# An adaptive-layer-norm transformer block on one core: attention in units of sixteen heads by 128 queries, feed-forward in sixteen blocks of 128 rows

## The chip, the cores and the metric

The kernel runs on one core of a Trainium2 chip. TensorE (PE in the profile) multiplies matrices, VectorE (DVE), ScalarE (ACT) and GpSimd (POOL) work on tiles, SyncE (SP) issues the transfers. The metric is the device time in microseconds (us); the median of three runs of the kernel before is 1634.18 us (1631.97 to 1639.09).

## The reference

One block with 2048 rows x 512 columns, 32 heads of 16 that share one K and one V, and a gated feed-forward of width 1792:

```python
mod = (_silu(c) @ w_mod).reshape(c.shape[0], 6, 1, -1)
sa, ca, ga, sb, cb, gb = (mod[:, 0], mod[:, 1], mod[:, 2], mod[:, 3], mod[:, 4], mod[:, 5])
h = _layernorm(x) * (1 + ca) + sa
q, k, v = h @ wq, h @ wk, h @ wv                # 32 heads of 16 in q; one head in k and v
p = _softmax(q_head @ k.T * 16 ** -0.5)
x = x + ga * (concat(p @ v) @ wo)
h = _layernorm(x) * (1 + cb) + sb
x = x + gb * ((_sigmoid(h @ w_gate) * (h @ w_up)) @ w_down)
```

## The kernel before

**Precision.** Operands of most products are split into a high and a low fp16 part; a product is three terms (high by high, high by low, low by high). The exponentials P and V are f32.

**Attention.** The loop runs over 32 *units*. A unit is eight heads by 256 queries (`QU` = 256, `NU` = 4 units for each of `NQ` = 8 blocks of queries), and has 16 *steps*, one for each 128 keys: 512 steps in all. In a step TensorE makes four `sa` tiles (queries by 512 keys, for the maxima of the next unit, which VectorE takes: `a_tile`), four `st` tiles (keys by queries, of which ScalarE makes P: `st_tile`), and the sums of P by V into the bank `craw` (`pv`). ScalarE copies that bank into `cs` at a unit's end (`unit_end`); `place`, `recip` and `finish` bring it through DRAM into the layout of wo's operand, divided by the softmax's sum.

**Row halves.** TensorE works with 64 rows at a time in column tiles of 32 (`columns`, L152 to L154): while P by V uses one half of the rows, the other products use the other half, and the halves swap. At a swap `hand_over` (L166) sends a tiny matmul (`craw<-nought`) through, whose semaphore `turn` the other half waits for.

**Feed-forward.** Beside the attention each half step takes a *piece* (L1186) of the feed-forward of an earlier block of 256 rows: wo, gate and up, and down. One *term* is eight matmuls, 64 rows by 32 columns by 512, four on each row half. A `Couple` (L198) is two groups with a bank each, either two row tiles of 128 or gate and up of one tile; each sums one half of the rows into its own bank in the first leg, and changes sides in the second. `ffn_block` makes the groups of a block, `pick` and `pace` choose which comes next and how many terms a half step gets, and `defer(n, f)` sets a follow-up n steps later. wo becomes urgent 9 steps into the next block's units (`SKIP`). Its sum is evicted by VectorE (first tile) or ScalarE (second), then POOL adds x and normalises (`norm`, `norm2`), and SP transposes the fp16 rows (`h2r` into `h`); gate and up follow at least three steps (`HGAP`) after the last transpose. `g` is the gated product, transposed likewise, and down follows.

**Weights.** Gate and up are split on the chip once and written to DRAM (`wD`); `ask` and `drip` load them again from there for each block, 14 tiles of two transfers (`gw<-wD`), with seven buffers.

**Order.** On TensorE, VectorE, ScalarE and SP the program's order is kept (class `Ordered`, L143: all such instructions carry this line in the profile). Before the loop stands a hand-written list, `PLAN`: the normalisation of x, K, V, the first groups of q (`q`, `QA`, `QL`, stored to `qD` and loaded again as `qp` by `lq`), and the maxima of the first unit (`a` a product, `x` its maximum). Behind the loop the last block's wo, gate, up and down run as full 128-row matmuls (`alone`, L194), with gate and up in the transposed form `gu_cols`, and one down of the block before.

Of the kernel before, what the change touches and what calls it, by code (L numbers as in the profile page):

```python
# [24 lines left out]
QU = 256  # L25
# [4 lines left out]
NU = 4  # L30
# [34 lines left out]
EGAP = 6  # L65
HGAP = 3
CHAIN = 26
QRATE = 1.1
MOST = 3
LEAST = 2.0  # L70
HELD = 60
SWAP = 5
FRESH = 0.9
WSTEPS = 66
WLAST = 100
# [4 lines left out]
FIRST = 70  # L80
# [16 lines left out]
def adaln_mqa_glu_kernel(  # L97
# [100 lines left out]
    class Couple:  # L198
# [27 lines left out]
        def alone(self):  # L226
            for g in self.gs:
                g.alone()

# [336 lines left out]
    def blank(eng):  # L566
        qp = wp.tile([P, 4, QU], F16, tag="qp", name="qp", bufs=4)
        for j in (32, 96):
            eng.memset(qp[j:j + 32], 0.0)  # L569
        return qp  # L570

    def load_q(i):
        b, o = units[i]
        qp = blanks.pop(0) if blanks else blank(pool)
        for j in range(2):
            src = qD[:, o * P:(o + 1) * P, b * QU:(b + 1) * QU].rearrange("h (r j d) q -> j h d r q", j=2, d=DH)[j]
            for g, hl in ((0, 0), (1, 1), (2, 0)):
                spq().dma_start(qp[64 * j + 16 * g:64 * j + 16 * (g + 1)], src[hl])
# [3 lines left out]
    def get_q(i):  # L582
        if i not in qps:
            b, o = units[i]
            assert (b * QU // QB, o) in qdone
            load_q(i)
# [6 lines left out]
    def spot(n):  # L593
        return n // 16, n // 8 % 2, n % 2, n // 2 % 4

    def a_product(i, n):
        qp = get_q(i)
        if i not in mxs:
            mxs[i] = wp.tile([P, 8, 2, 4], F32, tag="mx", name="mx", bufs=2)
        kc, qt, j, r = spot(n)  # L600
        sa = sbank("sa")
        l_, r_ = qp[64 * j:64 * j + 64, r, qt * P:(qt + 1) * P], kp[64 * j:64 * j + 64, kc * 512:(kc + 1) * 512]
# [6 lines left out]
    def a_max(i, n, sa):  # L609
        kc, qt, j, r = spot(n)  # L610
        dve.tensor_reduce(mxs[i][:, 4 * j + r, qt, kc:kc + 1], sa, axis=AX.X, op=ALU.max)
# [9 lines left out]
    def max_end(i):  # L621
        m16 = wp.tile([64, 32], F32, tag="m16", name="m16", bufs=4)
        for u in range(2):
            dve.tensor_reduce(m16.rearrange("p (h t u) -> p h t u", t=2, u=2)[:, :, :, u], mxs[i][64 * u:64 * u + 64],
# [22 lines left out]
    def st_tile(i, t, pr, j, second):  # L647
# [5 lines left out]
        columns(s_, kp[64 * j:64 * j + 64, t * P:(t + 1) * P], qp[64 * j:64 * j + 64, 2 * pr:2 * pr + 2].rearrange("p r q -> p (r q)"),  # L653
# [27 lines left out]
    def unit_end(i):  # L681
# [8 lines left out]
        lD = dr.tile([2, 8, QU], F32, tag="lD", name="lD", bufs=3)  # L690
        raw = t32("raw")
        defer(1, lambda: place(b, o, cs, lD, raw))
# [3 lines left out]
    def place(b, o, cs, lD, raw):  # L696
        for j in range(2):
            sp1.dma_start(lD[0].rearrange("(p r j) q -> j p r q", j=2, r=2)[j],
                          cs[DH + 64 * j:64 + 64 * j:32].rearrange("p (r q) -> p r q", r=2))
        for g in range(8):  # L700
            p_, r_, j = g // 4, g // 2 % 2, g % 2
            hh = 2 * j + p_
            sp1.dma_start(raw[DH * g:DH * (g + 1), :QU], cs[32 * hh:32 * hh + DH, r_ * QU:(r_ + 1) * QU])
        defer(W1, lambda: recip(b, o, lD, raw))

    def recip(b, o, lD, raw):
        lc = wp.tile([P, DH], F32, tag="lc", name="lc", bufs=2)
        rc = wp.tile([P, DH], F32, tag="rc", name="rc", bufs=2)
        sp1.dma_start(lc, lD[0].rearrange("h (s e) -> (h s) e", e=DH))

        def recip2():
            dve.reciprocal(rc, lc)
            sp1.dma_start(lD[1].rearrange("h (s e) -> (h s) e", e=DH), rc)
            defer(1, recip3)

        def recip3():
            sp1.dma_start(raw[:, QU:], lD[1].unsqueeze(1).to_broadcast([8, DH, QU]))
# [4 lines left out]
    def finish(b, o, raw):  # L722
        a_ = a_tile_of()
        ah, al = a_[:, :QU], a_[:, QU:]
        keep(pool.tensor_tensor(raw[:, :QU], raw[:, :QU], raw[:, QU:], op=ALU.mult))  # L725
        pool.tensor_scalar(ah, raw[:, :QU], 1.0, 0.0, op0=ALU.mult, op1=ALU.add)
        pool.tensor_tensor(al, raw[:, :QU], ah, op=ALU.subtract)
# [577 lines left out]
```

## Time and profile before

| | |
|---|---|
| three runs | 1631.97, 1634.18, 1639.09 us |
| the profiled execution | 1629.06 us |
| its span in the trace | 1627.3 us |
| mean granted clock of TensorE | 0.993 |
| bytes moved by transfers | 140.22 MB, 86 GB/s over the span |
| start of the steps (first exponential of the long row of steps) | 105.8 us |
| end of the loop (first wo row behind it) | 1537.72 us |

The time of an execution is a little longer than the span, which goes from the first to the last instruction that the trace has. A row of the timeline gives a start, a duration, the engine, the line, the operation with out<-in and the shapes, and a count; TensorE's rows overlap, since matmuls are pipelined, so the price of a matmul is the distance of two starts. A row of a table of windows gives the window, its length, for each engine named in its head the busy time and the number of instructions, then the granted clock, the share of time that the transfer engines were busy, and GB/s.

### The profile page before, as it was taken

Reading aid. Unit: us, or ns where it says so; the run is one execution under the profiler, and the core shown is the slowest. Engines: PE = TensorE matmul, PEld = TensorE weight load, DVE = VectorE, ACT = ScalarE, POOL = GpSimd, SP = SyncE. Lnnn points to the kernel's source line nnn. Section 1 sums busy time; section 2 is a strip of 40 time slices with the busy share of each in tenths; the row PEclk is TensorE's granted clock in tenths of the full one; section 3 lists DMA queues with packets and bytes.
Section 4 is the critical chain, followed back from the end, with each engine's and each line's share of the span. In section 5 each row is a group of like instructions: output and inputs, shape, how many; then the busy total and the mean of one; then the engine's idle time right before and its main releaser. Section 6 shows DMA issues by size and latency. Waiting matters only on the chain.

```text
span 1627.3 us, 91846 instructions
## 1 busy us (share of the span) xinstructions
PE 1585.3 (97%) x41481; PEld 987.3 (61%) x41481; DVE 1417.1 (87%) x2400; ACT 1288.7 (79%) x2325; POOL 666.2 (41%) x827
## 2 busy tenths in 40 slices
PE   6899999999999999999999999999999999999998
PEld 3335554546666666666666666666666666665465
DVE  7789999999999999999999999999999999993041
ACT  4539998888888888888888888888888888888600
POOL 5453877244425332443226232543226322533223
PEclk9979999999999999999999999999999999999999
DMA  7122554044521233114321433115411343124411
GB/s 238 71 84 65 164 156 131 28 118 106 139 68 29 75 97 108 31 39 130 92 63 33 89 85 106 30 38 128 112 42 42 81 121 85 23 60 107 116 65 52
DMA packets 185076, 140.22 MB, mean 86 GB/s; under 512 B 96372, under 2 KB 144492, under 8 KB 184684
## 3 DMA queue, kind: packets, MB, share of 16 engines
q1 hardware_dynamic: 184684, 134.34, 30.4%
q8 instruction: 325, 5.32, 1.3%
q14 instruction: 67, 0.55, 0.1%
HBM read 97.18 MB, written 16.24 MB: 70 GB/s over the span
## 4 chain that ended last, share of the span: by engine, by line
PE 88%; DVE 4%; ACT 2%; DMA 2%; POOL 1%; issue 1%; SPq 1%; POOLq 0%; ACTq 0%; DVEq 0%
PE craw L143 24%; PE sa L143 18%; PE pgu L143 17%; PE st L143 11%; PE pd L143 8%; PE po L143 2%; PE pgu L194 2%; PE pq L143 2%; PE pd L194 2%; DVE mx L143 2%; ACT th L143 1%; DMA lc<-lD 1%; SPq L143 1%; DMA xall<-in_A_x_dram 1%; ACT P L143 1%
## 5 line engine op out<-in xcount | busy, mean ns | idle before, releaser
L143 DVE TENSOR_REDUCE mx<-sa 128x1 f32<-128x512 f32 x2048 | 1299.8, 683 | 69.6 <-PE sa L143 33.2
L143 ACT ACTIVATE P<-st 128x512 f32<-128x512 f32 x2048 | 1179.3, 598 | 204.7 <-PE st L143 143.7
L143 PE MATMUL craw<-P,V 64*32 64x512 f32 x8192 | 1086.0, 597 | 1.0 <-ACT cs L143 1.0
L143 PE MATMUL st<-qp,kp 64*32 64x512 f16 x8192 | 832.7, 379 | 7.3 <-ACT P L143 6.1
L143 PE MATMUL sa<-kp,qp 64*32 64x512 f16 (+1 forms) x7940 | 827.9, 378 | 8.2 <-DVE mx L143 6.2
L143 PEld LDWEIGHTS <-kp 64*32 64x32 f16 x8192 | 323.1, 91 | 249.2 <-issue 79.1
L143 PE MATMUL pgu<-gw,h 64*32 64x512 f16 x9408 | 407.4, 376 | 3.2 <-DMA gw<-wD 1.2
L143 PEld LDWEIGHTS <-qp 64*32 64x32 f16 (+1 forms) x7940 | 270.2, 92 | 149.1 <-issue 58.7
L143 PEld LDWEIGHTS <-h 64*32 64x32 f16 (+1 forms) x9600 | 212.7, 92 | 77.8 <-issue 22.6
L143 PEld LDWEIGHTS craw<-P,V 64*32 64x32 f32 x8192 | 184.4, 105 | 21.7 <-issue 2.6
L143 PE MATMUL pd<-wdh,g 64*32 64x512 f16 x2688 | 136.1, 376 | 0.7
L952 POOL TENSOR_SCALAR th<-th 128x512 f32<-128x512 f32 x49 | 30.2, 617 | 246.4 <-ACT th L143 223.2
L569 POOL MEMSET qp<- 32x1024 f16 x60 | 56.7, 944 | 118.6 <-PE st L143 100.5
L143 PEld LDWEIGHTS <-g 64*32 64x32 f16 x4032 | 82.0, 92 | 31.0 <-issue 6.5
L725 POOL TENSOR_TENSOR raw<-raw 128x256 f32<-128x256 f32 x31 | 22.7, 733 | 160.6 <-DMA raw<-lD 151.7
L143 PE MATMUL pd<-wdl,g 64*32 64x512 f16 x1344 | 80.5, 376 | 0.0
L953 POOL TENSOR_TENSOR th<-th,u 128x512 f32<-128x512 f32 x49 | 62.8, 1282 | 4.1
L1009 POOL TENSOR_TENSOR ot<-ot,gb 128x512 f32<-128x512 f32 x12 | 15.4, 1281 | 114.3 <-ACT ot L143 114.3
L143 DVE COPY u<-pgu 128x512 f32<-128x512 f32 (+1 forms) x49 | 31.6, 644 | 34.9 <-PE pgu L143 34.8
L143 PE MATMUL craw<-nought 64*32 64x1 f16 x357 | 58.2, 163 | 1.1 <-issue 1.1
L956 POOL TENSOR_TENSOR gr<-th,gr 128x512 f16<-128x512 f32 x49 | 57.1, 1165 | 4.1
L143 PE MATMUL pq<-h,wdh 64*32 64x512 f16 (+1 forms) x688 | 54.4, 390 | 0.1
(156 smaller groups left out, 1112.5 us busy)
## 6 DMA issues: line engine op xcount, KB each, us to landing
gw<-wD SPq DMA_DIRECT2D x224, 256.0 KB
wD<-gw SPq DMA_DIRECT2D x28, 256.0 KB
wm<-in_w_mod_dram SPq DMA_DIRECT2D x6, 1024.0 KB
qp<-qD SPq DMA_DIRECT2D x192, 32.0 KB
qD<-q SPq DMA_DIRECT2D x16, 256.0 KB
xr<-in_A_x_dram SPq DMA_DIRECT2D x16, 256.0 KB
out_dram<-ot SPq DMA_DIRECT2D x16, 256.0 KB
raw<-cs SPq DMA_DIRECT2D x248, 16.0 KB
```

Of the source, the lines that this page charges most:

```text
L143: return (lambda *a, **k: keep(f_(*a, **k))) if pinned else f_
L194: pe.matmul(cut[0](self.bank) if cut else self.bank, l_, r_, start=(n == 0), stop=(n == self.n - 1))
L569: eng.memset(qp[j:j + 32], 0.0)
L725: keep(pool.tensor_tensor(raw[:, :QU], raw[:, :QU], raw[:, QU:], op=ALU.mult))
L952: pool.tensor_scalar(th, th, 1.0, 1.0, op0=ALU.add, op1=ALU.mult)
L953: pool.tensor_tensor(th, th, u_, op=ALU.mult)
L956: pool.tensor_tensor(rows[:, 1], th, rows[:, 0], op=ALU.subtract)
L1009: pool.tensor_tensor(ot, ot, mods[5], op=ALU.mult)
```

## The change

The units become sixteen heads by 128 queries: still 32 units of 16 steps with the same matmuls for the attention, but two units, not four, make up a block, and the blocks have 128 rows, sixteen in all. So the feed-forward of a block starts after 32 steps, not 64, and the weights are loaded sixteen times instead of eight. wo, the last quarter of gate and up (`rest`) and down have a single row tile; a new class, `Halves`, gives each half of the rows its own bank for that tile, without a swap, and the two banks are evicted by VectorE and ScalarE and added on POOL. The other gates and ups stay Couples, gate and up of one tile. Down of a block runs after the next block's first gate and up (`block`). `place` goes through a DRAM tile `rD` with four transfers and a load, where it was eight. Behind the loop the transposes are TensorE's (`turn_alone`). Several constants and `PLAN` differ.

```diff
-QU = 256
+QU = 128
-NU = 4
+NU = 2
-    'T00 m0 S12 T01 H00 S13 E00 T02 E01 H01 L00 T03 ra1 S20 H02 E02 L01 rb1 q000 H03 E03 pk00 L02 rc1 q001 L03 pk01 '
-    'N10 q002 N11 N12 q003 N13 pk02 QA00 S21 pk03 S22 T10 QL00 KB0 S23 T11 wh1 KL0 ra2 T12 S30 H10 rb2 T13 S31 E10 '
+    'T00 m0 S12 T01 H00 S13 E00 T02 E01 wh1 H01 L00 T03 ra1 S20 H02 E02 L01 wl1 rb1 q000 H03 E03 pk00 L02 rc1 q001 '
+    'L03 pk01 N10 q002 N11 N12 q003 N13 pk02 QA00 S21 pk03 q010 q011 q012 q013 S22 T10 QL00 KB0 QA01 QL01 S23 T11 '
...
-EGAP = 6
+EGAP = 4
-CHAIN = 26
-QRATE = 1.1
+CHAIN = 24
+QRATE = 1.5
-WSTEPS = 66
-WLAST = 100
+WSTEPS = 60
+WLAST = 66
+LLATE = 2
-FIRST = 70
+FIRST = 60
...
+    class Halves:
...
+            for n in range(n0, n1):
+                for j in (1 - side[0], side[0]):
+                    columns(self.banks[j], *self.term(n, slice(64 * j, 64 * j + 64)), n == 0, n == self.n - 1)
...
+            if n1 == self.n:
+                self.end(*self.banks)
...
-        qp = wp.tile([P, 4, QU], F16, tag="qp", name="qp", bufs=4)
+        qp = wp.tile([P, 8, QU], F16, tag="qp", name="qp", bufs=4)
...
+        for hh in range(4):
+            j, p_ = divmod(hh, 2)
+            sp1.dma_start(rD[p_].rearrange("(r j d) q -> j d r q", j=2, d=DH)[j],
+                          cs[32 * hh:32 * hh + DH].rearrange("p (r q) -> p r q", r=4))
...
+        def wo_end(pa, pb):
+            t1, t2, xr = t32("t1"), t32("t2"), x1["x"]
+            dve.tensor_tensor(t1, pa, mods[2], op=ALU.mult)
+            act.activation(t2, pb, AF.Identity)
+
+            def norm():
+                pool.tensor_tensor(t2, t2, mods[2], op=ALU.mult)
+                pool.tensor_tensor(xr, t1, xr, op=ALU.add)
+                pool.tensor_tensor(xr, t2, xr, op=ALU.add)
+                defer(2, norm2)
+
+            def norm2():
+                row_norm([t1], [xr], later=True)
+                pool.tensor_tensor(t1, t1, mods[4], op=ALU.mult)
+                pool.tensor_tensor(t1, t1, mods[3], op=ALU.add)
+                h2["t"], go = turned(parts_of(t1, 512), "h2", 8)
+                defer(HLATE, go)
+
+            defer(1, norm)
...
+        def last_end(pa, pb):
+            sa_, sb_ = t32("u"), t32("th")
+            act.activation(sa_, pa, AF.Identity)
+            dve.tensor_copy(sb_, pb)
...
+        def down_end(pa, pb):
+            ot, o2 = t32("ot"), t32("o2")
+            dve.tensor_tensor(ot, pa, mods[5], op=ALU.mult)
+            act.activation(o2, pb, AF.Identity)
...
-            first_, rest = ffn_block(b - 1)
+            first_, pairs_, rest_, down_, _ = ffn_block(b - 1)
             first_.ready = i * NKB + SKIP
             urgent.append(first_)
-            work.extend(rest)
+            block = [pairs_[0], *downs[-1:], *pairs_[1:], rest_]
+            downs.append(down_)
...
+            work.extend(block)
```

How the terms of the feed-forward and of q lie on TensorE, by a count of its rows in the two programs (a term is eight matmuls in the loop, one full matmul behind it):

| steps | before | after |
|---|---|---|
| 0 to 63 | 120 | 151 |
| 64 to 95 | 41 | 113 |
| 96 to 479 | 1665 | 1652 |
| 480 to 511 | 142 | 130 |
| behind the loop | 360 | 282 |

In the loop 28 of 357 hand-overs go. Behind it 20 transposes on TensorE are new (28, were 8). The first gate and up of a block stand 8 steps behind the last term of its wo, where they stood 11 behind.

SP's order ahead of the loop, from the first store of q on; `qD` is q in DRAM, `qp` the operand of the scores, `wm` the modulation's weights. Before:

```order
L551 DMA qD<-q_337 128x2x512
L578 DMA qp<-qD 16x4x256 x6
L143 DMA wm<-in_w_mod_dram 128x4x512 x4
L551 DMA qD<-q_616 128x2x512
L578 DMA qp<-qD 16x4x256 x6
L551 DMA qD<-q_1029 128x2x512
```

and after:

```order
L582 DMA qD<-q_316 128x2x512
L582 DMA qD<-q_351 128x2x512
L609 DMA qp<-qD 16x8x128 x6
L143 DMA wm<-in_w_mod_dram 128x4x512 x4
L582 DMA qD<-q_647 128x2x512
L582 DMA qD<-q_1015 128x2x512
L609 DMA qp<-qD 16x8x128 x6
```

Each of the first two units now needs two groups of q in DRAM; the loads have pieces of 128 elements instead of 256.

SP's order between a unit's end and the transposes of the normalised rows (`h`) in the middle of the loop; `lD`, `rD`, `lc`, `rc` and `raw` belong to the softmax's division. Before:

```order
L143 DMA lD<-cs 4x1x256 x2
L143 DMA raw<-cs 16x256 x8
L143 DMA lc<-lD 128x16
L143 DMA qp<-qD 16x4x256 x6
L143 DMA_TRANSPOSE h_33206<-h2r 128x4x128 x2
L143 DMA_TRANSPOSE h_33330<-h2r 128x4x128 x2
```

and after:

```order
L143 DMA lD<-cs 8x1x128 x2
L143 DMA rD<-cs 16x4x128 x4
L143 DMA gw<-wD 128x1024 x3
L143 DMA lc<-lD 128x16
L143 DMA gw<-wD 128x1024 x2
L143 DMA qp<-qD 16x8x128 x6
L143 DMA_TRANSPOSE h_37473<-rows 128x4x128 x2
```

There is one row tile with two transposes instead of two with four, and loads of weights stand between.

SP's last rows, behind the loop; `xr` is x again, `ot` the output tile. Before:

```order
L852 DMA xr<-in_A_x_dram 128x512 x2
L1016 DMA out_dram<-ot 128x512 x2
L830 DMA gw<-wD 128x1024 x10
L830 DMA gw<-wD_173 128x1024 x4
L1016 DMA out_dram<-ot 128x512 x2
```

and after:

```order
L905 DMA xr<-in_A_x_dram 128x512
L865 DMA gw<-wD 128x1024 x2
L865 DMA gw<-wD_149 128x1024 x4
L865 DMA gw<-wD 128x1024 x14
L1012 DMA out_dram<-ot 128x512
L865 DMA gw<-wD 128x1024 x8
L1012 DMA out_dram<-ot 128x512
L865 DMA gw<-wD 128x1024 x2
L865 DMA gw<-wD_149 128x1024 x4
L1012 DMA out_dram<-ot 128x512
```

More of the weights are loaded behind the loop, and two stores of finished rows stand ahead of the last loads.

More of the change, by code (lines that the diff above doesn't have):

```diff
@@ L1059, in adaln_mqa_glu_kernel @@
+        down.needs = [((b, f"g{p}"), GAP) for p in range(NPR)] + [((b, f"g{NPR}"), -99)]
+        return first, pairs, rest, down, norm_alone
     alist = [(i, n) for i in range(len(units)) for n in range(64)]
@@ L1096, in adaln_mqa_glu_kernel @@
     first.clear()
+    downs, late = [], []
     pctx.close()
@@ L1139, in places, with ready @@
         return [k - z for z, k in zip([0] + ends, ends)]
+    def ready(s, g):
+        return all(k in marks and s >= marks[k] + z for k, z in getattr(g, "needs", ()))
     def pick(s):
@@ L1143, in pick @@
             return urgent.pop(0)
-        if work and all(k in marks and s >= marks[k] + (EGAP if k == (0, "h21") else HGAP if k[1] == "h21" else GAP) for k in getattr(work[0], "needs", ())):
-            return work.pop(0)
+        for z in range(min(2, len(work))):
+            if ready(s, work[z]) and (z == 0 or "dn" in (work[0].stage, work[1].stage)):
+                return work.pop(z)
     def pace(s, g):
@@ L1172, in plan @@
         if sizes is None:
[L1173 to L1179 removed]
+            (urgent if g.stage == "wo" else work).insert(0, g)
+            return
         at = 0
```

461 lines of the change are left out of this document (212 added, 249 removed), and 20 rows, old and new, of the table PLAN.

## The prediction

> **What bounds the kernel now.** I read the page first (engines, slices, the share of the chain), then windows by stage, then the timeline and the chain at the places where the change acts.
>
> ```profile
> PE 1585.3 (97%) x41481; PEld 987.3 (61%) x41481; DVE 1417.1 (87%) x2400; ACT 1288.7 (79%) x2325; POOL 666.2 (41%) x827
> PE   6899999999999999999999999999999999999998
> PE 88%; DVE 4%; ACT 2%; DMA 2%; POOL 1%; issue 1%; SPq 1%; POOLq 0%; ACTq 0%; DVEq 0%
> ```
>
> TensorE is busy 97% of the span and is 88% of the chain that ended last. But the mean hides stages. The loop makes one exponential tile four times a step, so the count of P tiles on ScalarE divided by four is the number of steps in a window (columns: window, length, busy us and counts of PE, weight loads and ACT, clock, DMA share, GB/s; only rows of tile P):
>
> ```profile
> 105.80:276.20 170.40, 133.69 (x1000) 20.27 (x1000) 144.60 (x257) 0.97 0.42 123
> 276.20:361.90 85.70, 67.82 (x516) 10.57 (x512) 71.30 (x129) 1.00 0.27 79
> 276.20:296.10 19.90, 16.86 (x132) 2.53 (x128) 17.36 (x33) 1.00 0.21 60
> 361.90:1443.40 1081.50, 814.11 (x6152) 138.69 (x6144) 889.91 (x1537) 1.00 0.30 76
> 1443.40:1536.10 92.70, 66.78 (x516) 14.11 (x512) 72.86 (x128) 1.00 0.43 109
> ```
>
> So a step takes 170.40/64 = 2.66 us in steps 0 to 63, 85.70/32 = 2.68 in 64 to 95, 1081.5/384 = 2.816 in 96 to 479 and 2.90 in the last 32. The third row is a stretch of eight steps without any feed-forward work: 2.49 a step. There the maxima fill VectorE (same window, tile mx), while in the long stage TensorE does (same columns, all engines: PE, PEld, DVE, ACT, POOL):
>
> ```profile
> 276.20:296.10 19.90, 19.27 (x33) 1.00 0.21 60
> 361.90:1443.40 1081.50, 1076.39 (x32090) 718.49 (x32081) 1031.97 (x1717) 931.09 (x1682) 414.52 (x486) 1.00 0.30 76
> ```
>
> 19.27 of 19.90 us are VectorE's in the first, 1076.4 of 1081.5 us (99.5%) TensorE's in the second. **VectorE sets the early steps, TensorE the late ones**; a term of the feed-forward is dear late and cheap early.
>
> **The change part by part.** The price of a term (eight matmuls, both row halves) late in the loop:
>
> ```profile
> 1060.95 0.46 PE L143 MATMUL pd<-wdh,g 64*32 64x512 f16 x8
> 1061.16 0.46 PE L143 MATMUL pd<-wdl,g 64*32 64x512 f16 x8
> 1061.38 0.41 PE L143 MATMUL sa<-kp,qp 64*32 64x512 f16 x4
> 361.90:1443.40 1081.50, 349.98 (x8136) 27.69 (x43) 27.57 (x55) 1.00 0.30 76
> 361.90:1443.40 1081.50, 168.68 (x4032) 8.18 (x12) 7.11 (x12) 1.00 0.30 76
> 361.90:1443.40 1081.50, 49.57 (x1152) 4.09 (x6) 3.55 (x6) 1.00 0.30 76
> ```
>
> Starts lie 0.215 us apart: that is a term. The last rows (tiles pgu, pd, po) hold 8136 + 4032 + 1152 = 13320 matmuls, 1665 terms, 4.34 a step. By a count of the two programs' TensorE rows the terms stand so, before and after: steps 0 to 63, 120 and 151; 64 to 95, 41 and 113; 96 to 479, 1665 and 1652; 480 to 511, 142 and 130; behind the loop 360 and 282 full matmuls.
>
> *Steps 0 to 95, 103 more terms.* They start earlier because a block is 128 rows and the first is ready half as late. A TensorE step without terms is 2.816 − 4.34 × 0.215 = 1.88 us; with after's 2.4 and 3.5 terms it is 2.40 and 2.64, still under the 2.66 and 2.68 measured. The cover is VectorE. A straight line from 2.49 (no terms) to 2.816 (4.34) gives 2.755 for 3.5 terms, so 32 × 0.077 = +2.5; the first 64 steps, likewise, +2. Bounds: 0, and 103 × 0.215 = +22 if nothing is covered. I take **+4.5**.
>
> *Steps 96 to 479.* 13 terms fewer: −2.8. 28 fewer hand-overs (the tiny matmul into craw at which the halves swap sides) in all:
>
> ```profile
> 1063.57 0.48 PE L143 MATMUL pd<-wdl,g 64*32 64x512 f16 x6
> 1063.67 0.16 PE L143 MATMUL craw<-nought 64*32 64x1 f16 x1
> 1064.10 0.41 PE L143 MATMUL sa<-kp,qp 64*32 64x512 f16 x3
> ```
>
> By the pitch, sa was due two slots after 1063.57, at 1064.00; it starts at 1064.10, so a hand-over costs 0.1: **−2.8** (0 to −4.5, by the matmul's own 0.16). In return wo, the rest and down each leave two banks that VectorE and ScalarE empty, where a block of 256 rows left ten banks per 64 steps and now there are twelve: some 22 more tiles on VectorE, 0.644 each:
>
> ```profile
> L143 DVE COPY u<-pgu 128x512 f32<-128x512 f32 (+1 forms) x49 | 31.6, 644 | 34.9 <-PE pgu L143 34.8
> ```
>
> That is 14 us on an engine with 1081.5 − 1032.0 = 50 us free here. I take **+2** (0 to +14) with the turnover of the banks. The 224 more weight loads,
>
> ```profile
> gw<-wD SPq DMA_DIRECT2D x224, 256.0 KB
> PE pgu L143 <- DMA gw<-wD: 0.3, 1, 0.3
> ```
>
> double this row; the DMA share was 0.30, and TensorE waited for them 0.3 us in the stage (second row: engine and tile, what it waited for, us, times, longest): 0 (0 to +5).
>
> *The chain from wo to the first gate and up.* Before, the rows of the first tile run so:
>
> ```profile
> 1037.94 0.68 DVE L143 TENSOR_TENSOR t<-po,ga 128x512 f32<-128x512 f32 x1
> 1053.62 1.17 POOL L883 TENSOR_TENSOR h2r<-t,h2r 128x512 f16<-128x512 f32 x1
> 1056.33 2.84 SPq L143 DMA_TRANSPOSE h<-h2r  x2
> ```
>
> From the eviction to the last transpose's issue: 1059.2 − 1037.9 = 21 us. Now the first gate and up stand 8 steps behind wo, 8 × 2.82 = 22.6 us, where they stood 11 behind (31 us). SP's order puts six loads of qp and five of weights ahead of the transposes. With one tile there is one POOL addition more and one whole normalisation fewer. I take **+3** (0 to +28, that is 2 us in each of 14 blocks).
>
> *Steps 480 to 511*: 12 terms fewer, **−2.6**.
>
> *Behind the loop.* The chain there (start, us, what):
>
> ```profile
> 1537.72 4.06 PE po L194 x18
> 1541.78 1.90 PE craw L143 x16
> 1543.70 0.61 ACT cs L143
> 1544.35 1.99 PE pr L748 x8
> 1546.34 7.77 PE pd L194 x36
> 1611.39 7.78 PE pd L194 x36
> 1619.20 0.70 DVE ot L1011
> 1619.97 1.26 POOL ot L1015
> 1565.60 1.04 PE L1028 MATMUL pt<-ident,t 128*128 128x128 f32 x8
> ```
>
> A full matmul is 7.77/36 = 0.2158. From 1537.72 to 1619.18 it took 81.5. After: 282 × 0.2158 = 60.9, craw 1.9, cs 0.65, pr 2.0 (16 narrow ones side by side or one by one: 1 to 4), 28 transposes at 1.04/8 = 0.13, 3.6, of which eight were there; the wait for h2 before its first gate and up 1.3, and 0.8 where the last turned tile is awaited: 71.2, so **−10.3**. The last addition moves from POOL (1.26) to VectorE (0.70): **−0.6**. SP issues the stores of two finished blocks ahead of the last weight loads, and a store waits for its sum: **+2** (0 to +6).
>
> *Before the loop.* q of the second group of heads is now needed for the first unit:
>
> ```profile
> 26.09 1.09 ACT L143 ACTIVATE q<-pq 128x512 f32<-128x512 f32 x2 [2.66 <-PE pq L143]
> 27.26 1.17 POOL L143 TENSOR_TENSOR q<-q,q 128x512 f16<-128x512 f32 x1 [3.26 <-ACT q L143]
> 30.77 3.58 SPq L578 DMA_DIRECT2D qp<-qD  x6
> 36.92 0.60 PE L143 MATMUL sa<-kp,qp 64*128 64x512 f16 x3
> 40.35 1.28 DVE L143 TENSOR_REDUCE mx<-sa 128x1 f32<-128x512 f32 x2
> ```
>
> One group more through ScalarE (1.09) and POOL (1.17) and a second store put the first sa at 41 to 42 instead of 36.9, but VectorE's first maximum came at 40.35 anyhow, behind its own work; a group fewer stands in the part that follows, and the second unit's q is loaded later: **+2** (−1 to +6).
>
> The Trainium skill, "DMA: Bandwidth & Descriptors", section Specifications, wants transfers of 512 B or more and has a read-modify-write below. The pieces of qp go from 512 to 256 B here, against the change. In before the six loads end their issue at 34.35 and sa starts 2.6 later; were that doubled for both first units, it would add an estimated 5 us, and no run here shows 256-byte loads of this kind.
>
> **The sum**: 4.5 − 2.8 − 2.8 + 2 + 3 − 2.6 − 10.3 − 0.6 + 2 + 2 = −5.6, on the profiled execution's 1629.06 (span 1627.3): 1623.4. That execution lies 5.1 under the median of 1634.18, so against the runs: **1628**.
>
> **The rivals.**
>
> *B, early terms are free and nothing new is late.* Terms under 2.66 a step cost nothing (−4.5), the chain holds (−3), the stores and evictions cost nothing (−4): −17, so 1617. For it: 2.40 and 2.64 are below the measured steps. Against: the early steps are uneven, and 2.68 was an average with eight steps of 2.49 in it. The Trainium skill ("Trainium Kernel Development and Optimization", section Performance Expectations) calls matmul busy time a bad measure of how near a kernel is to its limit, and weight loads a better one: 718.49 of 1081.5 us is 66%, which would leave TensorE room for more terms than slots. Here the starts 0.215 apart, with no gap, speak against it.
>
> *C, the gain is eaten at the start.* The first block's gate and up wait for weights that are still on their way through DRAM, since blocks now start after 32 steps and not 64 while the weights are split at nearly the old pace (one job per 60 steps' share, was 66), or the first unit comes later: +5 to +6 on the sum, 1634, no change.
>
> *D, slower: h2 comes late.* The chain from wo to h2 takes over the 22.6 us that the order leaves, and TensorE stands still, once in each of 14 blocks that lie in the loop. It decides where the transposes land later than 22.6 us after wo's last matmul. At 2 us late it is +28 in place of +3: 1653; at 1 us, 1639. For it: 21 us measured, plus a landing. Against: the second tile of before was no better off,
>
> ```profile
> 1062.56 1.17 POOL L883 TENSOR_TENSOR h2r<-t,h2r 128x512 f16<-128x512 f32 x1
> ```
>
> it was ready 9 us after the first, with its gate and up some 8 us later than they stand now, and among the waits of TensorE in that stage none names h2.
>
> *That the change doesn't do what it says* would be that the terms don't move; the order excludes it.
>
> **How the numbers follow.** The sum as it stands 0.50 (0.21 of it below −0.5%, 0.29 within), B 0.18, C 0.10, D 0.22 (0.20 slower, 0.02 within). About 0.5%, 8.2 us, is what a measurement of this kernel tells from no change. Faster 0.39, same 0.41, slower 0.20. The range takes in B with some more of the open bounds (1606) and most of D (1652).
>
> **What would show it.** The windows by P counts: steps 64 to 95 at 2.75 each (2.68: B; over 2.85: C). Steps 96 to 479 at 2.81; over 2.85 with TensorE rows that wait for DMA h2 is D. The chain behind the loop some 71 us, with no wait for gw. The first sa by 42. The prediction is wrong if evictions of the second banks hold up VectorE's maxima (DVE over 97% in the long stage), or if early steps take 2.9 or more.

## The result, and the profile after

The changed kernel takes **1662.88 us** (median of 6 runs, 1659.26 to 1663.57), the kernel before 1633.71 (6 runs, 1631.97 to 1639.09): a ratio of 1.0168, 95% interval 1.0148 to 1.0187. It is 29 us slower where 6 us faster was forecast, and lies 11 us above the range, which ended at 1652. The profiled execution took 1663.57 us, span 1661.8, so 34.5 over the profiled one of before. The first was the slowest of its six runs and the second quicker than all six of before, so some 5 us of the differences between these two traces are the luck of the executions.

The page of after (engines; busy tenths of TensorE, and its granted clock, in 40 slices; what was read from HBM):

```profile
PE 1601.6 (96%) x41875; PEld 989.8 (60%) x41875; DVE 1440.8 (87%) x2410; ACT 1302.8 (78%) x2346; POOL 710.2 (43%) x864
PE   6899997989999999999999999999999999999998
PEclk9879998999999999999999999999999999999999
HBM read 159.97 MB, written 20.30 MB: 108 GB/s over the span
```

A slice is 41.5 us. TensorE has two slices under 9 that before had not, the 7 from 249 us and the 8 from 332 us on, and its clock an 8 in the first of them. From HBM 97.18 MB were read in before. The windows, cut at the same steps as before (rows of P alone; the last is the time behind the loop):

```profile
114.80:247.10 132.30, 98.59 (x744) 16.39 (x744) 109.03 (x192) 0.97 0.43 122
247.10:302.60 55.50, 37.20 (x264) 6.35 (x256) 35.89 (x65) 0.88 0.55 172
302.60:400.70 98.10, 72.49 (x517) 12.62 (x512) 74.02 (x128) 0.97 0.42 111
400.70:1499.10 1098.40, 821.69 (x6150) 146.36 (x6144) 891.55 (x1536) 1.00 0.49 118
1499.10:1586.10 87.00, 67.28 (x520) 13.27 (x515) 72.83 (x128) 1.00 0.52 124
1586.10:1661.80 75.70, 3.29 (x30) 0.61 (x21) 0.28 (x1) 0.99 0.39 136
```

| stretch | before | after | difference | forecast |
|---|---|---|---|---|
| to the first exponential | 105.8 | 114.8 | +9.0 | +2 |
| steps 0 to 47 | 127.0 | 132.3 | +5.3 | } +2 |
| steps 48 to 63 | 43.3 | 55.5 | +12.2 | } |
| steps 64 to 95 | 85.7 | 98.1 | +12.4 | +2.5 |
| steps 96 to 479 | 1081.5 | 1098.4 | +16.9 | -0.6 |
| steps 480 to 511 | 92.7 | 87.0 | -5.7 | -2.6 |
| behind the loop | 91.2 | 75.7 | -15.5 | -8.9 |

So the two ends that were to gain gained more than forecast, and everything ahead of step 480 lost. By the prediction's own signs, steps 64 to 95 took 3.07 us each (over 2.85 was to be C), and steps 96 to 479 took 2.86 with no wait of TensorE for h, so this is not D; VectorE is at 95% there, under the 97% that was to show held-up maxima.

Steps 48 to 63 are a pause with a cause that can be read. The first block's wo is evicted at 252.5 us; these are the rows that follow it on POOL, VectorE, SP and TensorE (start, duration, idle time before and its releaser in brackets):

```profile
260.70 1.26 POOL L915 TENSOR_TENSOR xr<-t,xr 128x512 f32<-128x512 f32 x1
261.99 0.69 DVE L143 BATCH_NORM_STATS2 st<-xr 128x6 f32<-128x512 f32 x1 [3.75 <-POOL xr L915]
263.53 0.61 PE L143 MATMUL sa<-kp,qp 64*32 64x512 f16 x4 [3.71 <-DVE mx L143]
271.88 1.16 POOL L372 TENSOR_TENSOR wdl<-wst,wdh 128x512 f16<-128x512 f32 x1
273.13 0.25 POOL L388 TENSOR_SCALAR ve<-mv 128x1 f32<-128x1 f32 x1
283.04 2.63 SPq L143 DMA_TRANSPOSE h<-rows  x2
285.63 0.63 PE L143 MATMUL pgu<-gw,h 64*32 64x512 f16 x8 [4.30 <-DMA h<-rows]
```

POOL splits the down weights in these steps (wst, wdh, wdl). x1 is added at 260.7 only; VectorE, in its program's order, stands before the statistics for 3.75 us with the maxima behind it, and TensorE for 3.71. The statistics are ready at 262.9, but POOL takes its first row of the normalisation up at 273.1, behind the rest of one such job and three more; so the rows of h leave at 283 and TensorE waits again. Steps 64 to 95 have another such place:

```profile
365.71 1.26 POOL L990 TENSOR_TENSOR u<-u,th 128x512 f32<-128x512 f32 x1
367.01 0.42 ACT L143 ACTIVATE th<-u 128x256 f32<-128x256 f32 x1 [5.06 <-POOL u L990]
367.96 0.62 PE L143 MATMUL st<-qp,kp 64*32 64x512 f16 x4 [5.31 <-ACT P L143]
```

POOL adds rest's two banks behind the whole normalisation of the next block; ScalarE stands before the tanh of the sum with the exponentials behind it, and TensorE for 5.3 us. In the long stage no such wait stands out. What is more frequent there than in before are short pauses that no semaphore ends, such as this one in the middle of a group:

```profile
755.83 0.37 PE L143 MATMUL pgu<-gw,h 64*32 64x512 f16 x1
756.74 0.62 PE L143 MATMUL pgu<-gw,h 64*32 64x512 f16 x15 [0.53 <-issue]
```

### The profile page after: what moved, and what is told of

It reads as the page before. It is cut to its first block, busy times and chain, and to the rows that moved or that the text cites. A ratio compares the mean times of both kernels' runs of the same rounds, so it can differ in the third digit from the quotient of the medians.

```text
span 1661.8 us, 92905 instructions
## 1 busy us (share of the span) xinstructions
PE 1601.6 (96%) x41875; PEld 989.8 (60%) x41875; DVE 1440.8 (87%) x2410; ACT 1302.8 (78%) x2346; POOL 710.2 (43%) x864
## 4 chain that ended last, share of the span: by engine, by line
PE 87%; ACT 4%; DVE 3%; POOL 2%; issue 2%; DMA 1%; SPq 0%; ACTq 0%; POOLq 0%; DVEq 0%
PE craw L143 23%; PE pgu L143 18%; PE sa L143 17%; PE st L143 10%; PE pd L143 8%; PE pq L143 3%; PE po L143 2%; DVE mx L143 2%; PE pd L257 2%; PE pgu L194 2%; ACT P L143 2%; ACT th L143 1%; PE pk L143 1%; DMA wm<-in_w_mod_dram 0%; PE pmod L143 0%
## 5 line engine op out<-in xcount | busy, mean ns | idle before, releaser
L143 DVE TENSOR_REDUCE mx<-sa 128x1 f32<-128x512 f32 x2048 | 1300.9, 683 | 96.7 <-PE sa L143 41.5
L143 PE MATMUL craw<-P,V 64*32 64x512 f32 x8192 | 1100.5, 599 | 1.8 <-issue 1.3
L143 PE MATMUL sa<-kp,qp 64*32 64x512 f16 (+1 forms) x7940 | 840.7, 380 | 13.5 <-DVE mx L143 10.2
L143 PE MATMUL pgu<-gw,h 64*32 64x512 f16 x9600 | 423.9, 377 | 9.3 <-DMA h<-rows 5.0
L143 PE MATMUL pd<-wdh,g 64*32 64x512 f16 x2912 | 152.7, 376 | 2.4 <-issue 1.5
L967 POOL TENSOR_SCALAR th<-th 128x512 f32<-128x512 f32 (+1 forms) x57 | 32.3, 566 | 254.3 <-ACT th L143 243.6
L1020 POOL TENSOR_TENSOR o<-o,gb 128x512 f32<-128x512 f32 x13 | 16.7, 1282 | 166.1 <-ACT o L143 166.1
L968 POOL TENSOR_TENSOR th<-th,u 128x512 f32<-128x512 f32 (+1 forms) x57 | 65.3, 1146 | 4.8
L895 POOL TENSOR_TENSOR rows<-th,rows 128x512 f16<-128x512 f32 (+1 forms) x57 | 59.5, 1044 | 4.8
L143 PE MATMUL po<-woh,a 64*32 64x512 f16 x960 | 52.9, 377 | 1.9 <-ACT th L143 1.4
L143 DVE COPY u<-pgu 128x512 f32<-128x512 f32 x43 | 29.3, 681 | 26.1 <-PE pgu L143 26.1
```

The lines of the kernel that those rows point to most:

```text
L143: return (lambda *a, **k: keep(f_(*a, **k))) if pinned else f_
L895: pool.tensor_tensor(rows[:, n:2 * n], src, rows[:, :n], op=ALU.subtract)
L967: pool.tensor_scalar(th, th, 1.0, 1.0, op0=ALU.add, op1=ALU.mult)
L968: pool.tensor_tensor(th, th, u_, op=ALU.mult)
L1020: pool.tensor_tensor(o2, o2, mods[5], op=ALU.mult)
```

## The experiments

Lengths are of the same stretches, from one profiled execution of each kernel; "before" beside a single time is a run of before on the same chip. Two spreads have to be kept in mind. Ten traces share after's work ahead of the loop without fillers, and their first exponential comes between 110.5 and 114.8 us. And steps 96 to 479 took 1081.5 us in before, but 1092.0 and 1089.0 in the two runs of before in which only the work ahead of the loop was changed (experiment 8).

**1. The first block later.** The statistics of the first block's normalisation stand 8 steps behind the additions instead of 2:

```diff
-                defer(2, norm2)
+                defer(2 if b else 8, norm2)
```

> After, with the statistics of the first block's normalisation (and all that follows them) set 8 steps behind its additions instead of 2; the other blocks are left alone. Theory A (POOL, which still splits weights in steps 48 to 60, comes late to the first block; VectorE's statistics and then TensorE wait for it in program order, and the granted clock falls after each pause): steps 48 to 63 take about 45 us instead of 55.5 (43.4 in before), no wait of TensorE for h over 1 us, the clock is 1.00 from 250 to 300 us, the whole 8 to 12 us shorter less some 3 us for the terms that move later. Rival (these steps are long because more terms stand in them, or because of the transfers): 55.5 within 2 us.

Measured: 1668.10 us (before 1631.21); steps 48 to 63 took 58.2 us, which neither expectation had. VectorE's pause at step 52 was gone, but a longer one came: the statistics were taken at 270.4 us, and POOL's next row of the chain and TensorE's waits (us, times, longest) were

```profile
288.16 0.25 POOL L388 TENSOR_SCALAR ve<-mv 128x1 f32<-128x1 f32 x1
PE st L143 <- DMA qp<-mh: 16.4, 1, 16.4
```

The queue of POOL was not empty 8 steps later either, and SP, holding the transposes of h, had the rows of the maxima (qp<-mh) behind them. So POOL's queue decides here, and the distance alone does not help.

**2. The tanh of rest later.** In `last_end`, behind the addition of the two banks:

```diff
-                defer(1, go)
+                defer(4, go)
```

> After, with the tanh of a block's last gate (rest) 4 steps behind POOL's addition of its two banks instead of 1. Theory A (ScalarE reaches that tanh before POOL has added, because POOL is in the next block's normalisation; the exponentials and TensorE stand behind it): steps 80 to 87 take 22 to 23 us instead of 28.8, the clock stays at 1.00 after them, the whole 6 to 9 us shorter; steps 96 to 479 within 2 us of 1098.4. Rival (POOL is behind in any case, and another wait takes the place): steps 64 to 95 within 2 us of 98.1.

Measured: 1654.63 us (before 1631.21), 8 under after's median. Steps 64 to 95, and then 96 to 479 (all engines: PE, PEld, DVE, ACT, POOL; clock; DMA share):

```profile
300.70:390.40 89.70, 88.76 (x2452) 54.39 (x2443) 85.91 (x146) 77.90 (x141) 46.90 (x58) 1.00 0.55 144
390.40:1491.00 1100.60, 1092.35 (x31989) 723.02 (x31984) 1055.23 (x1729) 941.26 (x1692) 448.39 (x526) 1.00 0.46 116
```

The first take 89.7 us at a clock of 1.00 (98.1 at 0.97): the wait was what cost them. The long stage did not gain (1098.4 in after).

**3. POOL free for the first block.** The fourteen jobs that split the down weights go behind the first normalisation:

```diff
-                if wdone < nw - 4 and (wdone + 0.5) * WSTEPS > (s + 1) * (nw - 4):
+                if wdone < nw - 14 and (wdone + 0.5) * WSTEPS > (s + 1) * (nw - 4):
-                if wdone >= nw - 4 and s < WLAST + 3 * (wdone - nw + 4):
+                if wdone >= nw - 14 and s < 59 + 1.3 * (wdone - nw + 14):
```

> After, with the fourteen jobs that split the down weights set at steps 59 to 77 (ten of them stood at 46 to 60, four at 66 to 75), so that POOL has none of them while it normalises the first block. Theory A (POOL's queue makes the first block late): steps 48 to 63 take 44 to 47 us instead of 55.5, the wait of TensorE for h is gone, the clock is 1.00 there; steps 64 to 95 stay at 98 or lose up to 3 us to the jobs that are there now. The whole 8 to 12 us shorter. Rival (more terms and the transfers make these steps long): 55.5 within 2 us.

Measured: 1645.35 us (before 1637.80), 17.5 under after. The window of steps 48 to 63 (P alone) and POOL's rows of the normalisation:

```profile
243.00:284.90 41.90, 33.96 (x261) 5.49 (x256) 36.13 (x65) 1.00 0.60 172
255.01 0.25 POOL L388 TENSOR_SCALAR ve<-mv 128x1 f32<-128x1 f32 x1 [1.90 <-DVE mv L143]
257.13 2.09 POOL L400 TENSOR_SCALAR t<-xr,mv,rs 128x512 f32<-128x512 f32 x1
```

41.9 us instead of 55.5, at a clock of 1.00, though after's terms all stand in them: POOL now waits for the statistics, not they for POOL. Steps 64 to 95 took 102.2 (98.1), and TensorE waited there 3.5 us for the maxima and 5.0 for the exponentials: the jobs are in the second block's way.

**4. Both edits, of 2 and of 3.**

> After, with both edits that were seen to act: the down weights' jobs at steps 59 to 77, and the tanh of rest 4 steps behind POOL's addition. If the two pauses are independent, steps 48 to 63 take 42 us and 64 to 95 some 92 to 96 instead of 98.1 (102.1 with the jobs alone), the clock stays at 1.00 from 250 to 400 us, and the whole lies 24 to 28 us under after, near 1637: what is left against before is the lead-in and the steady stage. If POOL merely passes its backlog on, 64 to 95 stay at 100 or more.

Measured: 1651.74 us (before 1633.27). Steps 48 to 63 took 41.9, but 64 to 95 took 98.0, and 96 to 479 took 1102.9. Steps 48 to 95 gain 13.7 us against after, not the 22 of the two gains together. The expectation had 92 to 96 for 64 to 95 if the pauses are independent, and 100 or more if POOL merely passes its backlog on; the result lies between. TensorE's wait of 5.0 us for the exponentials is gone, but these stand there now (us, times, longest):

```profile
PE sa L143 <- DVE mx L143: 3.5, 1, 3.5
PE st L143 <- DMA qp<-mh: 2.6, 1, 2.6
```

The first goes back to VectorE, which stands 4.4 us before the second block's statistics until POOL has added x: POOL passes part of its backlog on.

**5. The weights' loads.** The low halves of the gate and up tiles are not loaded, and the term reads the high half:

```diff
-            for z in range(2):
+            for z in range(1 if i < NDC * NPR else 2):
-                return h2["t"][rs, 4 * h_ + k, :], gws[at + NDC * p + k][rs, 2 * w_ + m]
+                return h2["t"][rs, 4 * h_ + k, :], gws[at + NDC * p + k][rs, m]
```

> After, without the loads of the low halves of the twelve gate and up tiles of a block; the term that used them uses the high half once more, so the low part of these weights is left out of the computation. TensorE's work is the same, the bytes of the weights fall to 57%, about to those of before. Theory T (the doubled transfers slow the steady stage): steps 96 to 479 take 1098.4 - 8 or less. Theory E (the evictions of twice the banks and where they fall do): 1098.4 within 2 us.

Measured: 1641.23 us (before 1631.21), 21.7 under after. The long stage (all engines: PE, PEld, DVE, ACT, POOL; clock; DMA share), after and then this run:

```profile
400.70:1499.10 1098.40, 1088.36 (x31952) 721.88 (x31942) 1048.43 (x1729) 938.70 (x1693) 450.84 (x530) 1.00 0.49 118
395.30:1476.90 1081.60, 1076.59 (x31951) 722.31 (x31950) 1046.91 (x1730) 939.07 (x1694) 451.67 (x530) 1.00 0.34 85
```

The same instructions, 16.8 us less, and with them all that after lost in this stage against the profiled before. The evictions of twice the banks, VectorE's 1047 us of work and the chain to h2 are still there: they cost little. The size is less sure than the direction: the same edit on top of runs 3 and 4 (experiment 9) took 11.3 and 8.6 us off this stage. Of the 21.7 us of the whole, 4.3 lie ahead of the loop, where none of these loads runs. The edit takes away half of the transfers of these tiles and their bytes together, so it does not tell which of the two costs.

**6. Before with every load twice.** Each transfer of the weights is followed by one of the same bytes into a DRAM buffer that nobody reads:

```diff
...
+                loads.append((u, lambda gw=gw, src=src, z=z: (sp1.dma_start(gw[:, 2 * z:2 * z + 2], src[:, 2 * z:2 * z + 2]),
+                                                              sp1.dma_start(spare(), src[:, 2 * z:2 * z + 2]))))
```

> Before, with each of the 448 half-tile transfers of the gate and up weights followed by a second one of the same bytes into a scratch buffer in DRAM that nobody reads; nothing else is changed. Theory T (the bytes of the weights slow the steady stage, because other transfers, the instructions' own among them, come later): steps 96 to 479 take 1095 us or more (1081.4 in before, 1092.0 in before with the new list), the whole is 10 us or more longer, and TensorE shows more pauses that no semaphore ends. Rival (the doubled loads are free, it is after's own order that pauses): 1081 to 1092.

Measured: 1722.94 us (before 1637.80); steps 96 to 479 took 1168.5. Far more than expected, and not all of it is the bytes: SP also issues twice as much, and the maxima and their rows (qp<-mh) come late. But TensorE's waits (us, times, longest) also had

```profile
PE pgu L143 <- issue: 5.9, 8, 1.7
PE sa L143 <- issue: 5.8, 5, 1.7
PE st L143 <- issue: 4.8, 3, 1.8
```

**7. The same bytes at a lower rate.** Four transfers of 128 KB for each tile, one in a half step; and, on top of run 4, one and two of them in turn. Of the first:

```diff
-            for z in range(2):
-                loads.append((u, lambda gw=gw, src=src, z=z: sp1.dma_start(gw[:, 2 * z:2 * z + 2], src[:, 2 * z:2 * z + 2])))
+            for z in range(4):
+                loads.append((u, lambda gw=gw, src=src, z=z: sp1.dma_start(gw[:, z:z + 1], src[:, z:z + 1])))
```

> After, with each weight tile loaded by four transfers of 128 KB instead of two of 256 KB, still one in a half step: the same bytes at half the rate. Theory T with bursts (a transfer delays others while it runs, and fewer of them run at once): steps 96 to 479 take 1090 us or less instead of 1098.4. Theory T with bytes (each byte costs): 1098 within 4 us. If gate and up now wait for their weights, it is longer, and TensorE's waits name gw.

> As the run with both edits, with the weights in pieces of 128 KB, one and two in turn in successive half steps: 192 KB in a half step in the mean, where after has 256 and the run with small loads had 128. Theory T (what runs of the weights at once delays the instructions' own transfers): the pauses that no semaphore ends are fewer, steps 96 to 479 take 1080 to 1090 us, with no wait for gw over 2 us in all. Rival (the bytes alone): within 4 us of the run with both edits.

Measured: 1713.40 us (before 1637.80) and 1671.34 (before 1633.27); steps 96 to 479 took 1145.9 and 1119.2. Neither gained, since the weights came late. But the pauses of the kind shown above were gone. TensorE's waits in that stage of the first:

```profile
PE pgu L143 <- DMA gw<-wD: 41.9, 21, 4.6
PE po L143 <- ACT th L143: 1.2, 6, 0.2
```

A count over the traces, from 400 to 1440 us: pauses of over 0.5 us between two starts of matmuls that nothing released, the time lost in them over the pitch of a term (0.215 us), and how many of them ended 1.1 to 1.7 us behind the end of a packet of instructions (queue q8, kind "instruction" in the table of DMA queues, 16 KB each). Of these packets after has 328, one for every 256 matmuls and weight loads of TensorE, and in this stretch one in 4.4 us. The numbers in brackets are those of the experiments:

```
kernel                               pauses  us    behind a packet
before                                    2   1.4   2
before, after's list (8)                  5   3.5   5
before, fillers (8)                       6   3.9   6
after                                    13   7.3  13
after, run 1                             13  13.3  13
after, run 2                             11   6.7  11
after, run 3                             10   6.1  10
after, run 4                             14   8.3  14
after, run 4 with fillers (8)            15   8.2  15
after, run 3 with more fillers (8)       15  13.1  15
before, every load twice (6)             21  21.4  21
after, half weights (5)                   0   0     0
after, small loads (7)                    0   0     0
after, three quarters rate (7)            0   0     0
before, half weights (9)                  0   0     0
after, run 4 with half weights (9)        1   0.6   1
after, run 3 with half weights (9)        0   0     0
```

Every pause lies behind a packet in this way, where only 14% of after's time does. In after the packet behind which a pause ends came 4.6 to 6.9 us after the one before it, 5.8 in the median, against 4.3 for all packets. So TensorE most likely runs out of instructions where the loads of the weights are dense; that is by the time of the packets, and was not tried by changing the number of instructions. It covers 7.3 of the 17 us; how the rest is spread over shorter delays stays open.

**8. The lead-in and the clock.** Before with after's list; then fillers (matmuls without a reader) between the last 30 maxima ahead of the loop, in after (on top of run 4) and in before, and more of them in after (on top of run 3). Of the list, the place of the fillers (f):

```diff
-... mz a x a x a x a x ...
+... mz a x f a x f a x f a x f ...
```

> Before, with after's list of the work ahead of the loop and nothing else. Theory A (the list alone makes the lead-in longer: the second group of q ahead of the first maxima leaves TensorE with pauses, and a lower clock follows): the first exponential at 113 to 116 us instead of 105.8, the whole 7 to 10 us longer than before. Rival (it is the units' new shape, that is the 256-byte pieces of qp or the weights' jobs): 105.8 to 108.

> As the run with both edits, with 30 matmuls of 128x128x512 without a reader put between the last 30 maxima ahead of the loop, where TensorE waits for VectorE. If the clock falls there because TensorE pauses, it stays above 0.9 from 95 to 125 us (0.50 to 0.72 in after) and the loop's step 48 is reached 4 to 8 us earlier than in the run with both edits. If it falls for another reason, the clock falls as before, and the lead-in is as long or up to 3 us longer.

> After, with the down weights' jobs late, the 30 fillers, and besides four fillers ahead of the first product for the maxima and two behind each of the first fourteen maxima, where TensorE pauses between 30 and 50 us. If the low clock from 40 to 80 us (0.67 to 0.84 in after) comes from those pauses, it stays above 0.95 and the first exponential is at 107 to 110 us (114.8 in after, 110.9 with the jobs late). If the list's own chain through VectorE and ScalarE makes the lead-in long, it starts at 111 to 115 whatever the clock.

> Before, with the 30 fillers between its last 30 maxima ahead of the loop, as in the run of after that had them. There the clock stayed at 1.00 and steps 0 to 47 took 3.3 us less, with a lead-in 1.5 us longer. If the clock acts the same way here: 1.00 from 95 to 125 us instead of 0.50 to 0.91, steps 0 to 47 in 123 to 125 us instead of 127.0, the whole 1 to 4 us shorter than before. If it does not, the whole is 0 to 2 us longer.

Measured, in this order: 1643.73 us (before 1631.21), first exponential at 112.1; 1651.14 (before 1633.27), at 113.7; 1661.49 (before 1634.76), at 120.3; and 1634.62 (12 runs), a ratio of 0.9998 to before (0.9982 to 1.0013), at 114.8. TensorE from 95 to 125 us, in run 4 without and with the fillers:

```profile
95.00:125.00 30.00, 26.97 (x297) 0.72 0.46 137
95.00:125.00 30.00, 29.33 (x356) 1.00 0.46 134
```

The fillers keep the clock up, and steps 0 to 47 take 128.9 us instead of 132.2 (124.1 instead of 127.0 in before); but the lead-in is longer by 1.5 us in after (less than its spread), and over all nothing is gained. In before the clock from 95 to 125 us is 0.72 as well, so this fall is no part of the loss. That the list costs all of the 9 us is not shown: before with its own list and fillers only at its end also started at 114.8 us, in an execution with a clock of 0.66 to 0.94 from 30 to 80 us. More fillers made it later. Both runs of before here took longer in steps 96 to 479, 1092.0 and 1089.0 us, though nothing is changed there.

**9. What is left.** Run 4 with halved loads; before with halved loads in the blocks of the loop; run 3 with halved loads.

> After, with both edits of the first blocks (down weights' jobs late, rest's tanh late) and without the loads of the low halves of the twelve gate and up tiles (their term uses the high half again, so that low part is left out of the computation). If the pauses of steps 48 to 95 and the transfers of the weights are the two causes of the loss, what is left is the sum of the prediction without them: steps 96 to 479 take 1078 to 1084 us, 48 to 95 some 136 to 142, the whole 1622 to 1630 us, under before by 0.2 to 0.7%. If something else costs too (the evictions, the lead-in), it stays at 1634 or above.

> Before, without the loads of the low halves of the twelve gate and up tiles in the blocks that the loop computes (their term uses the high half again, so that low part is left out). If every byte of the weights costs, before gains too: after lost 17 us in steps 96 to 479 for 58 MB more, so 29 MB less should give some 8 us: 1071 to 1076 us there and the whole 0.3 to 0.6% under before. If the cost begins only where the transfers come as close together as in after, it is 1078 to 1084 and within 0.2%.

> After, with the down weights' jobs late and without the loads of the low halves of the twelve gate and up tiles (low part left out as in the runs before), but with the tanh of rest where after has it: the run with all three edits lost 13 us in steps 96 to 479 against the one with the halved loads alone (1094.3 and 1081.6), spread over the steps, and only the tanh differs there. If that tanh 3 steps later is what cost them: steps 96 to 479 take 1080 to 1086 us, 48 to 63 take 42, 80 to 95 some 50 to 54, the whole 1622 to 1632, under before by 0.2 to 0.8%. If the jobs late or chance made them, 1090 or more and no gain.

Measured: 1641.24 us, a ratio to before of 1.0032 (1.0017 to 1.0048); 1623.33, 0.9921 (0.9898 to 0.9945); 1636.91, 1.0002 (0.9986 to 1.0019). The long stage of the second and the third:

```profile
361.10:1438.30 1077.20, 1074.06 (x32087) 717.89 (x32078) 1031.56 (x1717) 931.13 (x1682) 415.33 (x486) 1.00 0.24 59
387.60:1469.90 1082.30, 1076.65 (x31958) 724.48 (x31947) 1046.83 (x1729) 939.27 (x1694) 450.72 (x530) 1.00 0.35 84
```

The first missed by its long stage, 1094.3 us; the third, with the tanh back in its place, had 1082.3 there, so the tanh three steps later seems to cost some 12 us in the twelve blocks of the stage; run 2 against after and run 4 against run 3 give 2.2 and 9.4. A count over the traces is steadier: in this stage, what distances of 0.25 to 0.5 us between two starts of matmuls have over the pitch of 0.215 us comes to 23.0 to 24.0 us in the four traces with the later tanh (runs 2 and 4, run 4 with fillers, run 4 with halved loads) and to 17.3 to 18.0 in five without it (after, runs 3 and 5, run 3 with more fillers, run 3 with halved loads). So some 6 us are shown. In the third, steps 48 to 63 are mended (42.0) and the long stage is; steps 64 to 95, at 103.6 us with the clock at 0.66 for 20 us, are not: TensorE waits there 5.7 us for the maxima and 4.6 for the exponentials. That is about why the forecast gain does not show. Of before the whole fell by 12.5 us, more than by either expectation; of its long stage's profile only 4.3, since the profiled execution of before was some 5 us quicker than its median. So before gains 12.5 us (9.0 to 16.7 by the interval) from 22 MB less (84 tiles by 256 KB). After gains 8.6 to 16.8 us in steps 96 to 479 from 38 MB less there (144 tiles). The loads cost before too, and no threshold is seen between the two.

No run with the whole computation was faster than before.

## Why the prediction was wrong

*The bound.* It held: TensorE is 99% busy in the long stage of after (1088.4 of 1098.4 us). But busy time hid the loss, since 1081.6 us were enough for the same instructions in run 5. Nor did a busy share tell which engine sets the pace: in the eight steps that the prediction gave to VectorE (19.27 of 19.90 us) TensorE is busy for 19.46 of 19.90.

*Steps 0 to 95, "+4.5".* Wrong by 25 us, the step that failed worst. It took the first block's start as a matter of terms only. Its chain runs through POOL, which splits weights just then, and the engines keep their order, so a late POOL stops VectorE's maxima and ScalarE's exponentials too. Rival C had "the weights are split at nearly the old pace" in it, but made the weights' way through DRAM the wait, and priced it at +5; rival D had the right wait (h2 late), but in each of 14 blocks. It came in the first alone, where POOL was full. Run 3 gives 13.6 us for steps 48 to 63; run 2 gives 8.4 for the tanh in 64 to 95; both edits at once give 13.7 for steps 48 to 95 together, so what POOL's backlog costs in the second block was moved and not removed. The cover for the terms held in 64 to 95, where 72 more terms cost 4.0 us in run 2. It was overrated in steps 0 to 47: their 29 more terms cost 5.3 us (4.8 between the two runs with fillers and a clock of 1.00), 0.18 each, nearly the late price of 0.215. By the prediction's sum TensorE needs some 117 us for these steps, which took 132.3; why the terms were not covered is not shown.

*The clock.* It had no place in the sum. It fell ahead of the loop and behind the pauses. In windows of 10 us (busy time of PE, clock, DMA share, GB/s), the first ahead of the loop:

```profile
100.00:110.00 10.00, 6.74 (x18) 0.72 0.64 181
260.00:270.00 10.00, 6.47 (x104) 0.66 0.88 271
290.00:300.00 10.00, 10.00 (x265) 0.89 0.56 189
370.00:380.00 10.00, 10.00 (x229) 0.80 0.11 23
```

It was 0.66 and 0.80 behind the pauses of 3.7 and 5.3 us, so a pause costs about half as much again: run 2 took 5.3 us of waiting away and steps 64 to 95 fell by 8.4. The Trainium skill, "TensorE: Matmul & The Clock Gate", section Part 1: The HAM clock gate, says that TensorE goes to half its clock after an idle window of about 3.4 us. The pauses of 3.7, 4.3 and 5.3 us agree. From 95 to 125 us the clock was 0.72 with TensorE busy for 26.6 of 30 us and no wait longer than 1.1 us, and fillers brought it to 1.00: there the trace has the fall without an idle window. But the 30 us are uneven: from 101.2 to 104.6 us, just ahead of the fall at 104.4, TensorE was busy for only 1.69 of 3.4 us. So the fall came behind 3.4 us that were half busy.

*Steps 96 to 479, "-0.6".* The terms, the hand-overs, the evictions and the chain sum to 1080.9; with halved loads, which bring the bytes back to about those of before, it is 1081.6, so these terms were sized well as a sum, though a match within 1 us is luck where three runs of before with the same long stage took 1081.5 to 1092.0. The term that failed is "the 224 more weight loads: 0 (0 to +5)": halving the loads gave 16.8 us, and 11.3 and 8.6 in the other two pairs. It was read from the wait of TensorE for gw, 0.3 us. But a load delays others than its reader: most likely the instructions' own transfers were among them, and their wait carries no tile's name.

*The ends.* Behind the loop -15.5 instead of -8.9. These are the rows of after's chain there:

```profile
1587.40 1.47 PE po L257 x6
1591.44 1.08 PE pr L779 x32
1656.87 0.70 DVE ot L1029
1657.59 0.69 DVE ot L1030
```

From the first wo to the last matmul 69.4 us (1587.4 to 1656.8) stand against 81.5: the sum said 71.2, with pr at 2.0, which measured 1.08. The stores cost nothing: from the last matmul to the end it took 5.0 us, not 8.1. Steps 480 to 511 gained 5.7 for 2.6.

*The lead-in, "+2 (-1 to +6)".* It measured +9.0 in this execution; the list in before gave +6.3, and before's own list, with fillers at its end only, came as late as after in an execution with a lower clock. Of ten traces with the same work ahead of the loop this is the longest, the shortest gives +4.7. The first sa came at 38.2 us, by 42 as foretold, and VectorE's first maximum at 42.1 instead of 40.35, so most of the loss arises later. Mis-sized, with its cause partly open.

*The 256-byte pieces of qp.* TensorE waited 1.8 us for qp<-qD ahead of the loop, where no such wait stands out in before, and not at all in the long stage; the prediction's estimate of 5 us did not show.

## What to carry to other kernels

Work that starts earlier meets what runs earlier: before moving a block ahead, look up what the engines on its chain do at that time, the idle-looking one (POOL at 41%) above all, and what stands behind each wait in program order. Transfers that no engine waits for can still cost: where a kernel is bound by TensorE and made of many small instructions, as here, price a doubled transfer by an experiment that halves it, not by the wait of its reader. A pause of TensorE of some 5 us cost half as much again in clock, so a single pause in one block is worth mending, and an edit that mends it must be tried in all blocks, since the same edit cost some 6 us in the others. And the same stage took 1081.5 to 1092.0 us in three runs of before that do not differ in it: repeat the unchanged kernel before a difference of that size is put down to an edit.

## What the hardware showed that was not expected

TensorE paused 13 times for 0.5 to 1.3 us in the long stage with nothing to wait for, each time 1.1 to 1.7 us behind the end of a 16 KB packet of instructions, and once in the six runs in which fewer bytes of the weights ran, or ran more slowly. The loads cost 0.2 to 0.45 us for each MB in after (8.6 to 16.8 us for 38 MB in the long stage) and 0.57 in before (12.5 for 22 MB, 0.41 to 0.76 by the interval), at a mean DMA share of 0.24 to 0.49. And TensorE's clock fell to 0.72 over 30 us in which it was busy for 26.6, behind 3.4 us in which it was busy for half the time.
